# One side stage of a two-stage kernel reordered: the first chunk's inverse transform set aside in SBUF and gated later, modulation weights in other homes, two convolution inputs requested sooner, a second product group on GpSimd

## The chip, the cores and the metric

The kernel runs on one core of a Trainium2 chip (trn2). TensorE is PE in the rows, VectorE is DVE, ScalarE is ACT, GpSimd is POOL and SyncE, which issues most transfers, is SP. The metric is device time in microseconds (us), the median of several runs; lower is better. All stretches are in us from the start of the span.

## The reference

With S = 2048 tokens, D = 640 channels and F = 1728, everything in float32:

```python
mod = silu(c) @ w_mod                      # (1,640) @ (640, 3840), six rows of 640
sa, ca, ga, sb, cb, gb = mod               # shift, scale, gate, twice
h = layernorm(x) * (1 + ca) + sa           # x = A_q, (2048, 640)
ks = shift_conv4(A_k, A_shift_k)           # four taps along the tokens, per channel
kv = ks * A_v
y = long_conv(kv, A_ssm_k) + kv * A_ssm_D  # causal, 2048 taps per channel, by a transform
x = x + ga * (h * y)
h = layernorm(x) * (1 + cb) + sb
x = x + gb * (gelu(h^T @ w1 + b1) @ w2 + b2)^T
```

Layernorm is along the 640 channels, so the row statistics of `x` need all of `x`; the long convolution is per channel; the last line multiplies along the tokens.

## The kernel before

The first half, to about 280 us, computes the line `x = x + ga * (h * y)` in five chunks of 128 channels (`for c in range(NC)`). The rest is the token MLP, in three-pass float32r products; the change does not touch it.

The long convolution of a chunk is a transform written as small matmuls, in four named steps. `step1(side, t)` (L218) transforms the signal (side 0, from the tile `x`) or the filter (side 1, from `p`), in four quarters t; each fills one PSUM buffer that ACT copies into `z`. `f2(g)` (L237), g = 0 to 7, multiplies `z` by the tables `w`, ACT copies the filter's half to `kt`, DVE multiplies the two spectra into `p` (two products of 128x512), and `add` combines them into `y` (two 128x256 operations on POOL; those of the last group are on DVE for all chunks but the first). `i2(r)` (L267), r = 0 and 1, goes back the first half of the way, from `y` through PSUM into `z`; `i1(half)` (L287) the second half, from `z` into PSUM. `gate(c, ps, half)` then multiplies the result with the modulated layernorm of that chunk, the tile A1 (in `aux`, columns 2048 to 4095), and POOL adds the product to the rows of `x`, which are held in `xa` and `xb`.

A1 comes from `a1_ops(c)` (L298): 16 ACT operations (x - mean) / deviation, called `ac`, and DVE operations that scale and shift with the mod rows G1 and G0, called `po`.

The chunks overlap. While chunk c passes through f2, DVE prepares the next signals: `kv_ops(g)` (L180) makes eight operations of 128x512 for each of four groups of rows g (taps, sums, the product with v), written to `x`. A list `fill` holds them and `dv(n)` runs n of them at a place in DVE's program. For chunk 2, prepared while chunk 1 is in f2, group 1 is POOL's (`late`) and groups 0, 2 and 3 are DVE's. The loop over g keeps two halves of `p` by turns: the products of group g overwrite what the addition of group g - 2 read.

Only the first chunk carries the start of the modulation. `load_q` (L527) gathers the rows of `x` with eight indirect transfers on POOL's queue, DVE takes the statistics (`bn_stats`, L594), `rstd` (L335) makes the deviations with a square root on ACT and a correction on DVE, `mod_part(ps, kk, place)` (L350) multiplies silu(c) with one fifth of three mod rows' weights into the PSUM buffer `tap`, `mod_sum` (L357) copies the three rows to SBUF, and `mod_row(i)` (L362) broadcasts one to 128 partitions; rows 0 and 1 become G0 and G1 on ACT, and row 2, the gate, is multiplied into both on DVE. The five fifths of the weights are loaded into `homes` (L536) by SP. The later mod rows are loaded the same way while chunk 3 ends, and are used in chunk 4.

Each engine runs its own program in the order in which the Python code calls it, and the order is all written by hand. An engine that waits holds up what stands behind it, and so does SP's queue: a transfer waits there until its target is free, and until the transfer eight places ahead in SP's list has landed. `perm(c)` (L169) brings the filter from `aux` into `p`, after POOL's `perm_add(c)` has added ssm_D to it. `load_ks(c)` loads the filter into `aux` columns 0 to 2047, where k of chunk 1 has lain before.

## Time and profile before

| | us |
|---|---|
| median of 3 runs | 663.41 (660.25 to 663.55) |
| the profiled execution's own time | 661.62 |
| its span | 659.8 |
| PE busy | 615.0 (93%) |
| DVE busy | 536.9 (81%) |
| ACT busy | 328.6 (50%) |
| POOL busy | 135.1 (20%) |

Busy time by stretch, with the TensorE clock that was granted (1.00 is full speed):

| stretch, us | what runs there | PE busy | DVE busy | ACT busy | POOL busy | clock |
|---|---|---|---|---|---|---|
| 0 to 58 | inputs, chunk 0 in step1 and f2 | 43.25 | 43.71 | 24.86 | 44.01 | 1.00 |
| 58 to 82 | chunk 1 in step1, chunk 0 in i2, mod parts | 21.35 | 20.80 | 13.03 | 4.11 | 1.00 |
| 82 to 100 | mod rows, chunk 0 in i1, its gate | 13.88 | 15.78 | 13.07 | 8.13 | 1.00 |
| 100 to 124 | chunk 1 in f2 | 20.08 | 23.55 | 13.73 | 19.20 | 1.00 |
| 124 to 148 | chunk 1 in i2 and i1 | 23.27 | 19.70 | 13.18 | 4.78 | 1.00 |
| 148 to 192 | chunk 2 | 42.52 | 38.60 | 25.89 | 15.38 | 1.00 |
| 192 to 236 | chunk 3 | 42.16 | 30.96 | 24.62 | 15.28 | 0.96 |
| 236 to 280 | chunk 4 | 39.61 | 37.21 | 25.18 | 10.07 | 0.96 |
| 280 to 342 | start of the MLP | 55.28 | 55.67 | 48.36 | 0.00 | 0.97 |
| 342 to 660 | MLP | 313.60 | 250.93 | 126.68 | 14.16 | 1.00 |

A row of a timeline gives the start, the duration, engine, line, operation, the tile written and those read, the count that was merged into the row, and in brackets the idle time before it and what ended that. The same work repeats from chunk to chunk, so a stretch of one chunk can be held beside the same stretch of another.

### The profile page before, as it was taken

Reading aid. Unit: us, or ns where it says so; the run is one execution under the profiler, and the core shown is the slowest. Engines: PE = TensorE matmul, PEld = TensorE weight load, DVE = VectorE, ACT = ScalarE, POOL = GpSimd, SP = SyncE. Lnnn points to the kernel's source line nnn. Section 1 sums busy time; section 2 is a strip of 40 time slices with the busy share of each in tenths; the row PEclk is TensorE's granted clock in tenths of the full one; section 3 lists DMA queues with packets and bytes.
Section 4 is the critical chain, followed back from the end, with each engine's and each line's share of the span. In section 5 each row is a group of like instructions: output and inputs, shape, how many; then the busy total and the mean of one; then the engine's idle time right before and its main releaser. Section 6 shows DMA issues by size and latency. Waiting matters only on the chain.

```text
span 659.8 us, 20919 instructions
## 1 busy us (share of the span) xinstructions
PE 615.0 (93%) x9061; PEld 582.7 (88%) x9061; DVE 536.9 (81%) x930; ACT 328.6 (50%) x538; POOL 135.1 (20%) x151
## 2 busy tenths in 40 slices
PE   6878878999999999879999999999999999999997
PEld 2767667899998997779897999999999999999997
DVE  5879889979889369889979866575899689888895
ACT  0654575746747456377885553345443143333331
POOL 5786048325036043000000000000000520000000
PEclk9999999999999899889999999999999999999999
DMA  9999298465525046260318352245922636346601
GB/s 182 213 339 403 67 188 170 107 113 134 88 68 181 4 107 206 49 142 11 65 33 229 111 148 70 63 123 159 291 80 65 194 108 183 111 122 182 182 31 40
DMA packets 172188, 88.46 MB, mean 134 GB/s; under 512 B 92126, under 2 KB 163328, under 8 KB 172096
## 3 DMA queue, kind: packets, MB, share of 16 engines
q1 hardware_dynamic: 163628, 80.29, 46.6%
q0 software_dynamic: 1408, 5.52, 2.1%
q10 hardware_dynamic: 7060, 1.32, 1.3%
q8 instruction: 71, 1.16, 0.8%
q14 instruction: 21, 0.17, 0.1%
HBM read 73.01 MB, written 14.09 MB: 132 GB/s over the span
## 4 chain that ended last, share of the span: by engine, by line
PE 64%; DVE 17%; DMA 6%; ACT 5%; POOL 4%; issue 3%; ACTq 1%; SPq 0%; DVEq 0%; POOLq 0%
PE pst L1253 16%; PE pst L940 12%; PE pst L448 7%; PE pst L1330 7%; PE pst L226 7%; PE pst L274 5%; PE pst L245 4%; DVE p L59 3%; PE pst L294 2%; POOL t L59 2%; DVE aux L59 2%; DMA y<-in_A_ssm_k_dram 1%; ACT z L283 1%; PE pst L996 1%; DVE sm L553 1%
## 5 line engine op out<-in xcount | busy, mean ns | idle before, releaser
L245 PE MATMUL pst<-z,w 128*64 128x64 f32 x2560 | 80.4, 223 | 12.7 <-DVE p L59 6.6
L245 PEld LDWEIGHTS pst<-z,w 128*64 128x64 f32 x2560 | 77.5, 138 | 16.2 <-issue 12.3
L232 ACT ACTIVATE z<-pst 128x1024 f32<-128x1024 f32 (+2 forms) x45 | 43.4, 978 | 38.8 <-PE pst L226 38.6
L59 POOL TENSOR_TENSOR y<-p 128x256 f32<-128x256 f32 x72 | 51.0, 739 | 32.3 <-DVE p L59 32.0
L59 DVE TENSOR_TENSOR p<-pst,kt 128x512 f32<-128x512 f32 x80 | 51.1, 682 | 7.7 <-ACT kt L249 4.2
L249 ACT ACTIVATE kt<-pst 128x512 f32<-128x512 f32 x40 | 23.9, 598 | 38.2 <-PE pst L245 18.7
L226 PE MATMUL pst<-v,p 128*64 128x128 f32 x640 | 36.9, 274 | 5.3 <-ACT p L171 3.9
L1253 PE MATMUL pst<-r_z,m_w 128*128 128x320 f32 x222 | 41.6, 310 | 0.1
L274 PEld LDWEIGHTS pst<-v,y 32*128 32x128 f32 x1280 | 38.0, 187 | 3.5 <-issue 3.1
L226 PEld LDWEIGHTS pst<-v,p 128*64 128x64 f32 x640 | 34.8, 137 | 6.9 <-ACT p L171 4.9
L274 PE MATMUL pst<-v,y 32*128 32x64 f32 x1280 | 39.9, 273 | 0.6 <-issue 0.5
L59 DVE TENSOR_TENSOR s_w<-s_w,s_w 128x768 fp32r<-128x768 f32 (+1 forms) x26 | 24.6, 947 | 18.9 <-ACT s_w L924 14.2
L924 ACT ACTIVATE s_w<-s_w 128x768 fp32r<-128x768 f32 (+1 forms) x26 | 21.8, 837 | 35.7 <-PE pst L940 10.8
L1241 ACT ACTIVATE m_w<-m_v 128x896 fp32r<-128x896 f32 x24 | 22.7, 951 | 32.3 <-PE pst L1253 16.8
L59 DVE TENSOR_TENSOR tap<-tap,kt 128x512 f32<-128x512 f32 x51 | 35.5, 697 | 1.3
L226 PE MATMUL pst<-v,x 128*64 128x128 f32 x512 | 32.4, 282 | 2.9 <-issue 1.7
L1253 PEld LDWEIGHTS pst<-r_z,m_w 128*128 128x128 f32 x222 | 34.8, 188 | 0.4 <-DVE m_w L59 0.4
L448 PE MATMUL pst<-r_z,wb 128*128 128x320 f32 x180 | 29.6, 322 | 4.3 <-DVE aux L59 2.7
L448 PEld LDWEIGHTS pst<-r_z,wb 128*128 128x128 f32 x180 | 28.1, 197 | 5.6 <-DVE aux L59 2.9
L226 PEld LDWEIGHTS pst<-v,x 128*64 128x64 f32 x512 | 29.2, 142 | 4.0 <-issue 2.5
L283 ACT ACTIVATE z<-pst 128x512 f32<-128x512 f32 x38 | 20.9, 646 | 20.2 <-PE pst L274 20.2
L59 DVE TENSOR_TENSOR m_w<-m_v,m_w 128x896 fp32r<-128x896 f32 x24 | 27.9, 1167 | 3.3 <-ACT m_w L1241 2.9
(365 smaller groups left out, 1545.7 us busy)
## 6 DMA issues: line engine op xcount, KB each, us to landing
m_x<-xs SPq DMA_DIRECT2D x28, 160.0 KB
out_dram<-m_x SPq DMA_DIRECT2D x28, 160.0 KB
aux<-in_A_ssm_k_dram SPq DMA_DIRECT2D x8, 512.0 KB
m_v<-in_B_w_dram SPq DMA_DIRECT2D x9, 448.0 KB
in<-in_w_mod_dram SPq DMA_DIRECT2D x4, 960.0 KB
x<-in_B_w_dram SPq DMA_DIRECT2D x7, 448.0 KB
s_w<-in_B_w_dram SPq DMA_DIRECT2D x16, 192.0 KB
in<-in_A_v_dram SPq DMA_DIRECT2D x22, 128.0 KB
```

The lines of the kernel that those rows point to most:

```text
L59: TT = lambda eng, o, a, b, op: eng.tensor_tensor(o, a, b, op=op)
L226: pe.matmul(ps[64 * ri:64 * ri + 64, o:o + 255:2], lhs, F1[:, 128 * ri:128 * ri + 128], start=True, stop=True)
L232: act.activation(Z[:, side, t, :, k0:k1], ps.rearrange("p (a k e) -> p a k e", a=4, e=2)[:, :, k0:k1], AF.Copy)
L245: pe.matmul(ps[64 * h:64 * h + 64, o:o + 64], W2[k1 // 32][:, 2 * (k1 % 32) + ri], rhs, start=True, stop=True)
L249: act.activation(kt.rearrange("p (m i) -> p m i", i=32), pv[:, :, 1], AF.Copy)
L274: pe.matmul(pp[qd // 2][:, o:o + 64], Y[p, ri, i:i + 2].rearrange("p i k -> p (i k)"), V2[p, 64 * ri:64 * ri + 64], start=ri == 0, stop=ri ...
L283: act.activation(o, i, AF.Copy)
L448: pe.matmul(ps[0:m, h, 0:320], w_.bitcast(F32R), r_[:, 320 * h:320 * h + 320].bitcast(F32R), start=first and i == 0, stop=last and i == 2)
L940: pe.matmul(o, w_.bitcast(F32R), r_.bitcast(F32R), start=first and k == 0, stop=last and k == 2)
L1241: act.activation(W[n][0].bitcast(F32R), A[p, w_], AF.Copy)
L1253: pe.matmul(bank[n], w[:, i].bitcast(F32R), r.bitcast(F32R), start=i == 0 and k == 0, stop=i == 6 and k == 2)
L1330: pe.matmul(acc[s][:, h, 0:320], w[:, f_].bitcast(F32R), u[r + h].bitcast(F32R), start=f_ == 0 and k == 0, stop=f_ == NF - 1 and k == 2)
```

## The change

It has five parts, all in the first half.

1. POOL's queue before f2 of chunk 0: the taps of chunk 2 and the four small transfers of c, b2 and b1 go from POOL to SP, so the indirect gathers stand first on POOL. Two of five weight parts get other homes (`in` and `g` with `t`) and are requested before f2 of chunk 0; the third lies in `aux` from column 2048 on, so columns 0 to 2047 are free for the filter of chunk 1, which is requested (with k of chunk 2) right after step1 of chunk 1 begins.
2. Mod parts 0, 1 and 2 stand between the quarters of step1 on PE; the deviations are made before i2(1); a dummy Sqrt stands early on ACT.
3. The inverse of chunk 0 (`i1`) is copied by ACT into A1, in place of a DVE product from PSUM; the modulated layernorm of chunk 0 is written into the tile `x` instead (named XA). i1 and its copies stand ahead of `mod_row`; the gate is then `po`, a DVE product of two SBUF tiles, and POOL's addition.
4. Of the product groups of chunk 2, POOL takes 1 and 3, DVE 0 and 2. Seven operations of group 1 stand on POOL ahead of the gate's additions, its last behind them, then two of group 3; the other six stand in f2 of chunk 1. A one-column POOL operation ahead of group 1 reads DVE's copies of the table `v`.
5. The later mod weights are requested in nine pieces (`mod_third`) from f2 of chunk 3 on, each behind a one-column ACT write into its home, in place of three loads at the end of that chunk.

```diff
+    XA = X.rearrange("p (j d) -> p j d", j=16)
 def a1_ops(c):
+        A = A1 if c else XA
-        ac = [lambda j=j: act.activation(A1[:, j], XR(j, DC * c, DC), AF.Identity, scale=rs1[:, j:j + 1],
+        ac = [lambda j=j: act.activation(A[:, j], XR(j, DC * c, DC), AF.Identity, scale=rs1[:, j:j + 1],
...
-    homes = [T_v1[:, 2048:3968], T_in[:, 192:2112], T_aux[:, 0:1920], T_in[:, 2240:4160], P[:, 0:1920]]
+    homes = [T_in[:, 192:2112], None, T_aux[:, 2048:3968], T_in[:, 2240:4160], P[:, 0:1920]]
+    pl = [three(t) if t is not None else [G1, T_t[:, 0:640], T_t[:, 640:1280]] for t in homes]
-    load_taps(2, pool)
+    load_q((4, 5, 6, 7))
...
-        pool.dma_start(stg[o:o + t.shape[0], :], t)
+        sync.dma_start(stg[o:o + t.shape[0], :], t)
-    load_q((4, 5, 6, 7))
-    mod_load(0, 1, homes[1])
+    load_taps(2)
+    mod_load(0, 0, homes[0])
+    for j in range(3):
+        sync.dma_start(pl[1][j], dram(w_mod, 128 * 6 * D + 640 * j, [[6 * D, 128], [1, 640]]))
+    turns = {0: 6, 1: 7, 4: 8, 6: 0, 7: 1}
+    def mod_third(n):
...
+        kk, j = divmod(n, 3)
+        act.activation(pl[kk][j][:, 0:1], epsc, AF.Copy)
+        sync.dma_start(pl[kk][j], dram(w_mod, 128 * kk * 6 * D + 640 * (3 + j), [[6 * D, 128], [1, 640]]))
...
-                    mod_load(0, 0, homes[0])
-            if c == 1 and 1 < g < 6:
+            if c == 1 and g < 6:
                 late[g + 2]()
+            if cn == NC - 1 and g in turns:
+                mod_third(turns[g])
...
+            load_D(1)
             step1(0, 0)
...
+            act.activation(tm[:, 0:1], epsc, AF.Sqrt)
+            load_ks(1)
+            mod_part(tap, 0, pl[0])
+            load_halo(2)
+            load_k(2, 0, n=2)
             step1(0, 1)
+            mod_part(tap, 1, pl[1])
             i2(0)
             step1(0, 2)
+            mod_part(tap, 2, pl[2])
+            rstd(rs1, nm1, 0, 16)
...
+            pool.tensor_scalar(tm[64:128, 0:1], T_v1[64:128, 0:1], 1.0, None, op0=ALU.mult)
+            late = kv_ops(1, pool)
+            run(late[:7])
             i2(1)
-            k0 = step1(0, 3, True)
-            for kk in range(4):
+            step1(0, 3)
+            for kk in (3, 4):
                 mod_part(tap, kk, pl[kk])
...
+            run(ac[0:4])
             mod_sum(tap, T_kt[:, 0:640])
+            taps()
+            perm(1)
+            fill.extend(kv(3, ((0, 0), (2, 1, 2))))
+            dv(7)
+            for half in range(2):
+                act.activation(A1[:, 8 * half:8 * half + 8].rearrange("p j (y e c) -> p e (j y) c", e=2, c=2),
+                               i1(half).rearrange("p (e y c) -> p e y c", e=2, c=2), AF.Copy)
             for i in range(3):
                 mod_row(i, T_kt[:, 0:640])
             run(ac[4:16])
-            taps()
-            run(po[0:2])
-            perm(1)
-            fill.extend(kv(3, ((0, 0), (2,), (3, 1, 2, 3))))
+            for half in range(2):
+                y, x = A1[:, 8 * half:8 * half + 8], XH[half][:, :, 0:DC]
+                run(po[2 * half:2 * half + 2])
+                TT(dve, y, y, XA[:, 8 * half:8 * half + 8], ALU.mult)
+                TT(pool, x, x, y, ALU.add)
+            late[7]()
+            late = kv_ops(3, pool)
+            run(late[:2])
```

How this stands on the engines, at three places. First PE behind f2 of chunk 0: `pst<-v,x` is a quarter of step1 of chunk 1, `pst<-v,g` the transpose that carries c, `pst<-v,y` i2(0), and `tap<-` a mod part. Before:

```order
L226 MATMUL pst_740<-v,x 64x128 x16
L605 MATMUL pst_758<-v,g 128x36
L226 MATMUL pst_762<-v,x 64x128 x16
L274 MATMUL pst_780<-v,y 128x64 x2
L274 MATMUL pst_781<-v,y 128x64 x2
```

The same place on PE in the changed kernel:

```order
L227 MATMUL pst_744<-v,x 64x128 x16
L623 MATMUL pst_762<-v,g 128x36
L356 MATMUL tap<-in,sm 32x320 x6
L227 MATMUL pst_779<-v,x 64x128 x16
L356 MATMUL tap<-g,sm 32x320
L356 MATMUL tap<-t,sm 32x320 x2
```

Mod part 0, which reads silu(c), now stands ahead of the second quarter, and mod part 1 ahead of i2(0).

Second ACT, from the copies of i2(1) (`z<-pst`, 128x512) to the first copy of step1 of the next filter (`z<-pst`, 128x4x128x2, the last row of each): `sm<-sm 128x16` is the square root, `x<-xa` or `aux<-xa` is `ac`, `kt<-tap` is mod_sum, `tap<-rows` the taps, `p<-aux` perm(1), `g<-pst` the mod rows. Before:

```order
L283 ACTIVATE z<-pst_869 128x512 x2
L338 ACT_TABLE_LOAD
L338 ACTIVATE sm<-sm 128x16
L301 ACTIVATE aux<-xa,sm 128x128 x4
L358 ACTIVATE kt<-tap 96x640
L232 ACTIVATE z<-pst_938 128x4x128x2
L372 ACTIVATE g<-pst_1018 128x640
L374 ACTIVATE g<-pst_1022 128x640
L301 ACTIVATE aux<-xa,sm 128x128 x4
L301 ACTIVATE aux<-xb,sm 128x128 x8
L177 ACTIVATE tap<-rows 128x256
L171 ACTIVATE p<-aux 128x16x2x32 x2
```

In the changed kernel, where `aux<-pst` are the two new copies of i1:

```order
L284 ACTIVATE z<-pst_919 128x512 x2
L233 ACTIVATE z<-pst_988 128x4x128x2
L303 ACTIVATE x<-xa,sm 128x128 x4
L360 ACTIVATE kt<-tap 96x640
L178 ACTIVATE tap<-rows 128x256
L172 ACTIVATE p<-aux 128x16x2x32 x2
L662 ACTIVATE aux<-pst_1045 128x2x256x2
L662 ACTIVATE aux<-pst_1111 128x2x256x2
L374 ACTIVATE g<-pst_1177 128x640
L376 ACTIVATE g<-pst_1181 128x640
L303 ACTIVATE x<-xa,sm 128x128 x4
L303 ACTIVATE x<-xb,sm 128x128 x8
```

The taps, perm(1) and the two new copies stand ahead of the mod rows now; the square root is further up.

Third POOL, from the end of chunk 0's f2 into chunk 1's: `t<-in,t`, `t<-t` and `x<-t,in` are kv operations, `xa<-xa,aux` and `xb<-xb,aux` the gate's additions, `y<-p` the additions of f2. Before:

```order
L59 TENSOR_TENSOR aux<-aux,rows 1x64 x2
L59 TENSOR_TENSOR xa<-xa,aux 128x8x128
L59 TENSOR_TENSOR xb<-xb,aux 128x8x128
L59 TENSOR_TENSOR t<-in,t 128x512 x2
L59 TENSOR_TENSOR t<-t 128x512
L59 TENSOR_TENSOR t<-in,t 128x512
L59 TENSOR_TENSOR y<-p 128x8x32 x2
```

In the changed kernel, from the end of the seven operations of group 1 on:

```order
L59 TENSOR_TENSOR t<-t 128x512
L59 TENSOR_TENSOR xa<-xa,aux 128x8x128
L59 TENSOR_TENSOR xb<-xb,aux 128x8x128
L59 TENSOR_TENSOR x<-t,in 128x8x32x2
L59 TENSOR_TENSOR t<-in,t 128x512 x2
L59 TENSOR_TENSOR t<-t 128x512
L59 TENSOR_TENSOR t<-in,t 128x512
L59 TENSOR_TENSOR y<-p 128x8x32 x2
```

Between the gate's additions and the first addition of f2 stand five kv operations, where four stood; behind that the two lists agree to the end of chunk 1's f2.

More of the change, by code (lines that the diff above doesn't have):

```diff
@@ L586, in mixer_kernel @@
                 perm_add(cn)
+            if cn == NC - 1 and g in turns:
+                mod_third(turns[g])
+            if c == 1 and g == 5:
+                kv_loads(3, 3)
         pend_m()
@@ L664, in mixer_kernel @@
             dv(7 if cn is not None else 8)
+            if cn == NC - 1:
+                mod_third(2)
             i2(0)
@@ L682, in mixer_kernel @@
         if cn == NC - 1:
[L683 to L689 removed]
+            mod_third(5)
+        for half in range(2 if c else 0):
             ps = i1(half)
[L691 removed]
+            if half:
                 dv(3)
[L693 removed]
+            else:
                 k0 = step1(1, 0, True)
[L695 to L696 removed]
             gate(c, ps, half)
[L698 to L700 removed]
         spill(c)
```

54 lines of the change are left out of this document (18 added, 36 removed).

## The prediction

> **What bounds the kernel now.** I read the page first, for the span and the chain of waits.
>
> ```profile
> span 659.8 us, 20919 instructions
> PE 64%; DVE 17%; DMA 6%; ACT 5%; POOL 4%; issue 3%; ACTq 1%; SPq 0%; DVEq 0%; POOLq 0%
> ```
>
> PE carries the chain, but 17% of it is DVE, with POOL and ACT behind. The change touches the stretch from 36 to 124 us and chunk 3, so I took PE's timeline there next.
>
> ```profile
> 58.49 1.97 PE L226 MATMUL pst<-v,x 128*64 128x128 f32 x32 [0.83 <-DVE x L59]
> 68.29 1.91 PE L226 MATMUL pst<-v,x 128*64 128x128 f32 x30 [1.66 <-issue]
> 75.92 1.28 PE L354 MATMUL tap<-v,sm 128*32 128x320 f32 x12
> 80.25 1.25 PE L354 MATMUL tap<-p,sm 128*32 128x320 f32 x12
> 100.53 10.20 PE L245 MATMUL pst<-z,w 128*64 128x64 f32 x320 [0.49 <-ACT z L232]
> 120.20 3.71 PE L226 MATMUL pst<-v,x 128*64 128x128 f32 x64 [0.44 <-DVE p L59]
> 123.85 3.80 PE L274 MATMUL pst<-v,y 32*128 32x64 f32 x128
> 147.89 5.82 PE L245 MATMUL pst<-z,w 128*64 128x64 f32 x192 [0.49 <-ACT z L232]
> 163.95 3.69 PE L226 MATMUL pst<-v,x 128*64 128x128 f32 x64
> ```
>
> Three landmarks: chunk 1's step1 begins at 58.49, its f2 at 100.53 and its i2(0) at 123.85. What follows 123.85 the change leaves alone until chunk 3, so the gain is what i2(0) of chunk 1 moves, plus chunk 3. f2 took 19.67 us (100.53 to 120.20), and in chunk 2 16.06 (147.89 to 163.95), so other engines hold PE in chunk 1.
>
> **POOL's queue before f2 of chunk 0.** The waits of 34 to 60 us, then POOL's timeline:
>
> ```profile
> DVE p L59 <- POOL y L59: 3.4, 4, 1.7
> 35.95 1.09 POOL L152 DMA_DIRECT2D rows<-in_A_shift_k_dram  x2
> 39.42 1.03 POOL L531 DMA_INDIRECT xb<-in_A_q_dram,rows_of  x1 [0.30 <-issue]
> 42.66 0.94 POOL L531 DMA_INDIRECT xb<-in_A_q_dram,rows_of  x1 [0.94 <-DMA rows<-in_A_shift_k_dram]
> ```
>
> DVE's products wait for POOL's additions, which stand behind the gathers, and those behind six small transfers. Without these the first gather moves from 39.42 to 36.3 (0.30 of issue after 35.95), and the wait of 0.94 for the taps goes too. Then DVE sets the pace. Of its 3.4 us of waiting behind POOL nearly all goes, as 3.1 of transfers and 0.94 of wait leave POOL's queue ahead of it: I take 3.0 us, so step1 begins at 55.5. Ends: 0, if the gathers still hold the additions (everything below is then 3.0 later), and 3.4, the whole wait. SP takes the small transfers, which are read only when step1 begins.
>
> **PE and ACT up to the mod rows.** ACT's timeline:
>
> ```profile
> 62.95 0.21 ACT L607 ACTIVATE sm<-sm 128x5 f32<-128x5 f32 x1
> 74.11 2.21 ACT L283 ACTIVATE z<-pst 128x512 f32<-128x512 f32 x4 [2.82 <-PE pst L274]
> 79.53 1.65 ACT L301 ACTIVATE aux<-xa,sm 128x128 f32<-128x128 f32 x4 [1.59 <-DVE sm L343]
> 81.56 0.70 ACT L358 ACTIVATE kt<-tap 96x640 f32<-96x640 f32 x1 [0.38 <-PE tap L354]
> 84.29 0.70 ACT L374 ACTIVATE g<-pst 128x640 f32<-128x640 f32 x1
> 89.50 0.63 ACT L177 ACTIVATE tap<-rows 128x256 f32<-128x256 f32 x1
> 90.06 2.19 ACT L171 ACTIVATE p<-aux 128x1024 f32<-128x1024 f32 x2
> 93.27 1.09 ACT L232 ACTIVATE z<-pst 128x1024 f32<-128x1024 f32 x1 [1.02 <-PE pst L226]
> ```
>
> Mod part 0 needs silu(c), which ended at 63.16, 4.67 after step1 began. PE is done with the first quarter and the transpose after 2.1 and so waits about 2.65 that it did not wait before. Three mod parts now stand ahead of i2(1): 1.1 each (five in the 5.58 from 75.92 to 81.50), 3.3. The stall of 1.66 plus 0.25 in front of the third quarter has no releaser; I leave it out, and keep it for the upper end. i2(1) ended 15.6 after step1 began, where ACT's row at 74.11 was released; now 15.6 - 1.9 + 2.65 + 3.3 = 19.65, so at 75.15. Behind PE's new wait for silu(c) stand the other quarters and i2, and for those waits ACT.
>
> From there ACT is the chain, because the mod rows now stand behind everything: i2(1) 2.2, the last quarter 1.1, `ac` 1.65, mod_sum 0.7, taps 0.65, perm(1) 2.2, two copies of i1, mod rows 1.4. The copies are not in the trace: they move 128x1024 from PSUM like `z<-pst`, 1.09 each (nearest row; ends 1.09 and 1.23, the price of DVE's product below), so 2.2. Sum 12.1: G1 is there at 87.2, against 84.99. The dummy Sqrt takes a table load out of this chain and lies under PE's matmuls. Four more `ac` (1.64) put the first half of A at 88.8. The filter of chunk 1, which perm reads, is requested before step1's second quarter now, and has some 20 us to land.
>
> **The gate.** DVE's and POOL's timeline:
>
> ```profile
> 75.48 0.21 DVE L595 BATCH_NORM_AGGREGATE sm<-sm 128x2 f32<-128x12 f32 x1
> 79.53 2.46 DVE L622 TENSOR_SCALAR v<-v 64x2048 f32<-64x2048 f32 x2
> 86.55 2.52 DVE L59 TENSOR_TENSOR aux<-aux,g 128x1024 f32<-128x1024 f32 x2 [0.29 <-ACT aux L301]
> 89.17 1.23 DVE L59 TENSOR_TENSOR aux<-pst,aux 128x1024 f32<-128x1024 f32 x1
> 90.31 4.54 DVE L59 TENSOR_TENSOR aux<-aux,g 128x1024 f32<-128x1024 f32 x2
> 90.57 3.21 POOL L59 TENSOR_TENSOR xa<-xa,aux 128x1024 f32<-128x1024 f32 x1 [2.58 <-DVE aux L59]
> 96.33 2.37 POOL L59 TENSOR_TENSOR xb<-xb,aux 128x1024 f32<-128x1024 f32 x1 [2.55 <-DVE aux L59]
> ```
>
> Two DVE operations that took 2.52 took 4.54 while POOL's addition ran, and that addition 3.21 instead of 2.37: one engine stood while the other worked. The Trainium skill, "SBUF — State Buffer", section "SBUF: two separate sides", has a rule for it: a DVE operation with two SBUF inputs and a GpSimd operation that reads SBUF exclude each other for whole instructions. The trace agrees by the two rows above. By that rule the new product, from two SBUF tiles in place of PSUM and SBUF, joins the operations that exclude, and the sum is the next one only if POOL is idle when DVE's pair starts, and each POOL operation still running then adds its length.
>
> POOL's group 1 waits for DVE's copies of `v`, and the gate's additions stand behind it. The statistics end 3.0 earlier, at 72.7; the square root (0.3, its table loaded before) and DVE's correction (1.6, to 79.53 in the trace) follow, and the copies (2.46 and 1.23) end at 78.3. One table copy (1.1) and seven operations of 1.3 (98.66 below) end at 88.7, just as DVE's pair begins at 88.8. So 2.52 + 1.23 after 88.8 puts the first gate product at 92.5, against 90.40. From there the order of operations is as before, and from 90.40 to the end of POOL's second addition (98.70) it took 8.3. So POOL is through at 100.8, 2.1 later than before. f2 of chunk 1 itself can begin sooner: step1 of the filter needs perm and free PSUM, and ACT copies its quarters behind the twelve `ac` from about 92, so f2 begins near 95.5 instead of 100.53.
>
> **f2 of chunk 1.** From the groups of 100 to 124 us, and POOL's timeline:
>
> ```profile
> L59 POOL TENSOR_TENSOR y<-p 128x256 f32<-128x256 f32 x14 | 10.0, 743 | 2.9 <-DVE p L59 2.8
> L59 DVE TENSOR_TENSOR p<-pst,kt 128x512 f32<-128x512 f32 x16 | 10.1, 681 | 0.0
> 98.66 2.51 POOL L59 TENSOR_TENSOR t<-in,t 128x512 f32<-128x512 f32 x2
> 119.54 2.81 POOL L59 TENSOR_TENSOR y<-p 128x256 f32<-128x256 f32 x4 [1.01 <-DVE p L59]
> ```
>
> DVE never waited in this f2: it was the bound, with 16 kv operations among its products, and the change takes 8 away (0.7 each, 5.6) and does 7 more ahead of it. But POOL gets them. From 98.70 to 122.35 POOL took 23.65, 2.8 of it waiting for DVE. It now has one kv operation more (1.3; nine instead of eight) and no waits: 23.65 - 2.8 + 1.3 = 22.15, after 100.8, so 122.95. Every product of group g waits for the addition of group g - 2, and four kv operations of group 3 stand ahead of the first addition. So PE, five us early, is held by POOL through this f2. The last product and DVE's last addition follow, and i2(0) begins at about 123.5 instead of 123.85: gain 0.3. Ends: -1.6 with the stall of issue back, +2.5 (90.40 to 98.70 in 6.1 instead of 8.3) if POOL and DVE do not exclude each other once.
>
> **Chunk 3.**
>
> ```profile
> 203.14 3.99 SPq L347 DMA_DIRECT2D in<-in_w_mod_dram x2
> 211.98 1.32 PE L274 MATMUL pst<-v,y 32*128 32x64 f32 x34
> 213.83 3.22 PE L274 MATMUL pst<-v,y 32*128 32x64 f32 x94 [0.52 <-issue]
> 216.98 3.26 PE L226 MATMUL pst<-v,x 128*64 128x128 f32 x32
> 216.00:218.00 2.00, 2.00 (x35) 1.88 (x33) 1.99 (x4) 1.14 (x3) 0.00 (x0) 0.57 0.00 0
> ```
>
> Here the weights arrive in one burst; right behind it PE stalls 0.52 in i2(0), and the granted clock is 0.57 (the last number but two) in the two us shown. i2(0) took 5.07 (211.98 to 217.05) against 3.80 in chunk 1, and the quarter behind it 3.26 against 1.97: 2.55 together. Requested in pieces from 193 on, the burst is gone. The gain lies between 0 and 2.55; the stall of 0.52 I expect gone, of the slow clock I count half, as two later stretches (0.96 and 0.97 in the table above) have slow spells without such loads: 1.3. The Trainium skill, "TensorE: Matmul & The Clock Gate", section "What's actually happening", says that the clock is halved by a free-running activity window. The trace agrees in size (0.57); by that alone the loads would not matter and this term would be 0.5. The nine ACT writes (0.2 each by the 128x5 one above) fall where ACT waits for PE, and SP's queue behind them holds only chunk 3's writes to DRAM: nothing.
>
> **The sum.** 0.3 + 1.3 = 1.6 less: 660.0 against the profiled execution's 661.62. The median of three stands 1.8 above that one, and all four average 662.2. From this I take 661.0. A measurement can tell about 0.5% of this kernel, 3.3 us, from no change.
>
> **The rivals.** First, faster: POOL does not hold f2. If POOL's additions come in time, f2 runs at chunk 2's 16.06 from 95.5, and i2(0) starts at 95.5 + 16.06 + 3.7 = 115.3, 8.5 earlier; with chunk 3 some 652. For it speaks that PE is ready 5 us early and DVE relieved; against it, that POOL's 23.65 holds only 2.8 of waiting. In part it may come true, if POOL's chain begins before 98. Chance 0.2.
>
> Second, slower: the gathers of x come late. From the windows:
>
> ```profile
> 50.00:55.00 5.00, 3.98 (x118) 3.62 (x114) 3.84 (x7) 2.44 (x4) 4.67 (x7) 1.00 1.02 412
> ```
>
> The transfers run at their limit (share 1.02, 412 GB/s) while the gathers are under way, and a weight part (128 rows of 3x640, 0.98 MB, 2.4 us at that rate) is now requested ahead of most gathers. If bn_stats waits so much and the 3.0 of the first term is lost, it ends 5.4 later than I count, at 78.1. Then the square root on ACT holds the copies of i2(1), DVE's copies of `v` end at 83.7 instead of 78.3, and i1 and the mod rows move by 3.4. POOL's group 1, which reads those copies first, ends at 94.0 instead of 88.7, beside DVE's pair of SBUF inputs: 1.3 more of exclusion. i2(0) begins at 123.5 + 4.7 = 128.2, and the time is 664.7, or 666 without the gain in chunk 3. It decides from bn_stats ending after 75, where POOL's group 1 begins to reach into `po`. For it: the full share. Against: the gathers were never waited for by bn_stats before. Chance 0.2.
>
> Third, the change doesn't do what it says: the weights' pieces and the first term move nothing that PE waits for, and the other edits trade places: 661.6 to 663. Chance 0.1. The forecast has 0.5; its own range is 657.5 to 664.5.
>
> **The numbers.** Range 654 to 667: from the middle of the first rival to beyond the second. Faster by over 0.5%: the first rival and a fifth of the forecast, 0.31. Slower by over 0.5%: most of the second rival, 0.17. The rest, 0.52, within.
>
> **What would show it.** Right: step1 of chunk 1 begins at 55 to 56; PE waits 2 to 3 us for ACT ahead of mod part 0; POOL's second gate addition ends at 100 to 102, later than before; f2 of chunk 1 begins at 95 to 96 with PE waiting for DVE in it and DVE's products for POOL; i2(0) at 123 to 125. Wrong: f2 of chunk 1 in under 18 us would mean that POOL does not hold it; DVE idle in bn_stats for a transfer would mean the second rival; a clock of 1.00 in chunk 3 makes that term 2.5.

## The result, and the profile after

The changed kernel took 668.2 us (median of 20 runs, 663.0 to 676.8); the kernel before took 662.8 (20 runs). The ratio is 1.0065, 95% interval 1.0037 to 1.0094: slower by 0.65%, where 661.0 was forecast and 667 was the upper end of the range. Here and below medians are of all runs, ratios of the undisturbed ones. The profiled execution of the changed kernel took 671.65, with a span of 669.9 and a mean granted clock of 0.966; that of the kernel before had 659.8 and 0.992, and in it PE had no slow spell from 34 to 145 us, which none of the other 19 profiles of this study repeats.

The page's head and the shares of the chain in the changed kernel:

```profile
span 669.9 us, 20943 instructions
PE 65%; DVE 16%; ACT 6%; issue 4%; POOL 3%; DMA 3%; SPq 1%; ACTq 0%; POOLq 0%; DVEq 0%
```

The shares say little: the same engines as before. The places do. PE's timeline of the changed kernel at the landmarks of the prediction (start, busy, and in brackets the wait ahead of the row and what ended it):

```profile
36.74 5.82 PE L246 MATMUL pst<-z,w 128*64 128x64 f32 x192 [0.49 <-ACT z L233]
50.66 5.50 PE L246 MATMUL pst<-z,w 128*64 128x64 f32 x127 [2.54 <-issue]
58.76 1.97 PE L227 MATMUL pst<-v,x 128*64 128x128 f32 x32
63.47 1.46 PE L356 MATMUL tap<-in,sm 128*32 128x320 f32 x12 [2.56 <-ACT sm L625]
64.85 3.48 PE L227 MATMUL pst<-v,x 128*64 128x128 f32 x32
76.30 3.80 PE L275 MATMUL pst<-v,y 32*128 32x64 f32 x128
101.23 5.82 PE L246 MATMUL pst<-z,w 128*64 128x64 f32 x192 [0.49 <-ACT z L233]
115.00 5.50 PE L246 MATMUL pst<-z,w 128*64 128x64 f32 x128 [3.18 <-DVE p L59]
128.80 4.02 PE L275 MATMUL pst<-v,y 32*128 32x64 f32 x128 [0.51 <-DVE y L59]
```

step1 of chunk 1 begins at 58.76 (forecast 55.5; 58.49 before), f2 at 101.23 (95.5; 100.53 before) and i2(0) at 128.80 (123.5; 123.85 before). Three waits stand out: 2.54 without a releaser ("<-issue") in f2 of chunk 0, where the longest of the kernel before was 1.78, the forecast one for silu(c), 2.56, and 3.18 for DVE's products in chunk 1's f2. Behind each of the three, rows that should be short are long: step1's second quarter took 3.48 where the first took 1.97.

The windows of the changed kernel at those places (the last three columns are the granted clock, the transfers' share and their GB/s):

```profile
52.00:54.00 2.00, 2.00 (x44) 2.00 (x42) 0.00 (x0) 0.18 (x1) 1.01 (x2) 0.50 1.01 403
62.00:64.00 2.00, 0.53 (x6) 0.42 (x9) 1.93 (x8) 1.97 (x3) 0.00 (x0) 1.00 1.03 391
66.00:68.00 2.00, 2.00 (x22) 2.00 (x20) 1.93 (x7) 0.00 (x0) 0.00 (x0) 0.50 1.04 397
116.00:118.00 2.00, 2.00 (x43) 2.00 (x42) 1.92 (x3) 0.33 (x1) 2.00 (x4) 0.50 0.41 93
```

Each of the three waits is followed by a spell at half clock. The waits of 34 to 60 us in the changed kernel (engine, what it did, whom it waited for: us in total, times, longest):

```profile
ACT kt L250 <- issue: 4.2, 1, 4.2
PE pst L246 <- issue: 4.0, 3, 2.5
DVE p L59 <- POOL y L59: 0.3, 1, 0.3
```

DVE's wait for POOL, 3.4 before, is gone as forecast. But PE and ACT now stand longer without a releaser (PE 4.0 against 3.2), and step1 begins no sooner. In part that is this execution's later start: f2 of chunk 0 began at 36.74 instead of 34.90, so step1 stands 22.02 behind it instead of 23.59; but the second profile of the kernel before, below, has 21.75. The rest of the chain in the changed kernel's timeline, on ACT, DVE and POOL:

```profile
91.97 0.70 ACT L376 ACTIVATE g<-pst 128x640 f32<-128x640 f32 x1 [1.11 <-PE pst L367]
94.25 2.48 DVE L59 TENSOR_TENSOR x<-x,g 128x1024 f32<-128x1024 f32 x2 [0.60 <-ACT x L303]
96.76 1.23 DVE L59 TENSOR_TENSOR aux<-aux,x 128x1024 f32<-128x1024 f32 x1
97.91 4.52 DVE L59 TENSOR_TENSOR x<-x,g 128x1024 f32<-128x1024 f32 x2
98.12 3.22 POOL L59 TENSOR_TENSOR xa<-xa,aux 128x1024 f32<-128x1024 f32 x1 [4.85 <-ACT x L303]
103.83 2.39 POOL L59 TENSOR_TENSOR xb<-xb,aux 128x1024 f32<-128x1024 f32 x1 [2.49 <-DVE aux L59]
124.01 4.20 POOL L59 TENSOR_TENSOR y<-p 128x256 f32<-128x256 f32 x6
```

From the first gate product's end (97.99) to the end of POOL's second gate addition (106.22) it took 8.23, forecast 8.3; from there to the end of POOL's list (128.21) 22.0, forecast 22.15. Every step stands in its forecast order and length; the whole chain stands 5.4 too late.

### The profile page after: what moved, and what is told of

The parts are those of the page before. It is cut to its first block, busy times and chain, and to the rows that moved or that the text cites. A ratio compares the mean times of both kernels' runs of the same rounds, so it can differ in the third digit from the quotient of the medians.

```text
span 669.9 us, 20943 instructions
## 1 busy us (share of the span) xinstructions
PE 627.6 (94%) x9061; PEld 593.5 (89%) x9061; DVE 532.2 (79%) x922; ACT 330.8 (49%) x550; POOL 142.9 (21%) x154
## 3 DMA queue, kind: packets, MB, share of 16 engines
q8 instruction: 71, 1.16, 0.7%
## 4 chain that ended last, share of the span: by engine, by line
PE 65%; DVE 16%; ACT 6%; issue 4%; POOL 3%; DMA 3%; SPq 1%; ACTq 0%; POOLq 0%; DVEq 0%
PE pst L1281 16%; PE pst L968 11%; PE pst L450 7%; PE pst L1358 7%; PE pst L227 6%; PE pst L275 6%; PE pst L246 6%; PE pst L295 2%; DVE p L59 2%; POOL t L59 2%; ACT z L284 2%; PE pst L1024 1%; POOL y L59 1%; DVE x L59 1%; PE tap L356 1%
## 5 line engine op out<-in xcount | busy, mean ns | idle before, releaser
L246 PE MATMUL pst<-z,w 128*64 128x64 f32 x2560 | 81.9, 227 | 13.3 <-DVE p L59 6.9
L246 PEld LDWEIGHTS pst<-z,w 128*64 128x64 f32 x2560 | 79.7, 142 | 16.1 <-issue 11.7
L275 PEld LDWEIGHTS pst<-v,y 32*128 32x128 f32 x1280 | 41.0, 201 | 4.8 <-issue 3.4
L227 PE MATMUL pst<-v,p 128*64 128x128 f32 x640 | 39.8, 287 | 4.0 <-ACT p L172 4.0
L275 PE MATMUL pst<-v,y 32*128 32x64 f32 x1280 | 42.9, 287 | 0.6 <-DVE y L59 0.5
L227 PEld LDWEIGHTS pst<-v,p 128*64 128x64 f32 x640 | 37.9, 146 | 5.6 <-ACT p L172 4.8
L59 DVE TENSOR_TENSOR tap<-tap,kt 128x512 f32<-128x512 f32 x48 | 33.4, 696 | 1.2
L59 DVE TENSOR_TENSOR m_w<-m_v,m_w 128x896 fp32r<-128x896 f32 x24 | 27.9, 1167 | 3.3 <-ACT m_w L1269 2.9
```

What stands on the lines that cost most here:

```text
L59: TT = lambda eng, o, a, b, op: eng.tensor_tensor(o, a, b, op=op)
L227: pe.matmul(ps[64 * ri:64 * ri + 64, o:o + 255:2], lhs, F1[:, 128 * ri:128 * ri + 128], start=True, stop=True)
L246: pe.matmul(ps[64 * h:64 * h + 64, o:o + 64], W2[k1 // 32][:, 2 * (k1 % 32) + ri], rhs, start=True, stop=True)
L275: pe.matmul(pp[qd // 2][:, o:o + 64], Y[p, ri, i:i + 2].rearrange("p i k -> p (i k)"), V2[p, 64 * ri:64 * ri + 64], start=ri == 0, stop=ri ...
```

## The experiments

Four theories. **CHAIN**: the gate ends later and POOL's longer list holds chunk 1's f2. **CLOCK**: PE's new waits of 2.5 to 3.2 us bring half-clock spells. **FETCH**: the waits without a releaser, while the transfers are full, hold f2 of chunk 0, whatever POOL's queue holds. **PIECES**: the weights' pieces in chunk 3 cost time.

**The same again, and the pieces.** These runs are the changed kernel again, the same without the pieces, the kernel before with the pieces alone, and the kernel before again. The edit for the second, and its opposite for the third (in part):

```diff
-            if cn == NC - 1 and g in turns:
-                mod_third(turns[g])
...
-            mod_third(5)
+            for kk in range(2):
+                mod_load(3, kk, (T_in[:, 0:1920], T_in[:, 1920:3840])[kk])
+            for j in range(3):
+                sync.dma_start(pl[2][j], dram(w_mod, 256 * 6 * D + 640 * (3 + j), [[6 * D, 128], [1, 640]]))
```

> The changed kernel once more, for a second profile. Theory CHAIN (the gate of chunk 0 and POOL's list hold chunk 1): i2(0) of chunk 1 begins 4 to 5 us later than in the kernel before (123.85), at 127 to 129, and POOL's products' wait on it is there again. Theory CLOCK (PE's new waits make the granted clock drop): the same waits of 2.5 to 3.2 us on PE (for silu(c) near 61, for DVE's products near 112) are each followed by some 3.4 us at about 0.5, and the whole is 0.4 to 0.9% slower. If the slow spells lie elsewhere or are missing while the time is the same, CLOCK falls.

> The changed kernel with part 5 undone (the later mod weights in three loads at the end of chunk 3, as before). CHAIN: part 5 was worth 1.3 us at most 2.5, so this is 0 to 2.5 us slower than the changed kernel, some 0.8 to 1.0% slower than before. A third theory, PIECES (the nine pieces and ACT's one-column writes cost time in chunks 3 and 4): this is faster than the changed kernel by 2 us or more.

> The kernel before with part 5 alone (the later mod weights in nine pieces). CHAIN and the prediction: 0.5 to 2.5 us faster than before, i2(0) of chunk 3 without the stall. PIECES: slower than before by 2 us or more, with the slow clock in chunk 4. CLOCK: within 1 us of before, as no wait on PE is changed.

> The kernel before once more, for a second profile. CLOCK: no waits of over 2 us on PE between 36 and 124 us and a clock of 1.00 there; slow spells only from chunk 3 to the start of the MLP, at other places than in the first profile. CHAIN: i2(0) of chunk 1 within 1.5 us of 123.85, f2 of chunk 0 and step1 as in the first profile.

Measured: the changed kernel 668.64, ratio 1.0108 [1.0064, 1.0152]; without the pieces 669.05, 1.0112 [1.0066, 1.0157]; the pieces alone 662.74, 1.0020 [0.9985, 1.0054]; the kernel before 665.51 in one run. The pieces are worth nothing in time, so PIECES falls, and so does the prediction's 1.3. They do remove the stall in i2(0) of chunk 3: over all 20 profiles it is there in four of the seven without the pieces, as in the second one of the kernel before, and in none of the 13 with them, where i2(0) took 3.80.

```profile
218.23 2.90 PE L274 MATMUL pst<-v,y 32*128 32x64 f32 x94 [0.52 <-issue]
```

The slow clock behind it was the first execution's own: the quarter behind i2(0) took 3.26 there and 1.97 in the other 19. The second profile of the kernel before misses what was expected of it: three waits of 2.1 to 2.3 without a releaser, spells at half clock from 71 and 88 us, and i2(0) of chunk 1 at 128.94, as late as in the changed kernel. So one pair of profiles doesn't give the loss. Counted from the start of f2 of chunk 0, i2(0) of chunk 1 begins 89.0 and 90.1 later in the two profiles of the kernel before, 92.1 and 93.2 in the two of the changed one.

**CLOCK, twice, and CHAIN.** Two ways to end PE's wait for silu(c): mod part 0 behind the second quarter, or five useless matmuls in the wait; and group 3's kv operations given back to DVE (each in part):

```diff
# after_swap
+            step1(0, 1)
             mod_part(tap, 0, pl[0])
             load_halo(2)
             load_k(2, 0, n=2)
-            step1(0, 1)
# after_dummy
+            for _ in range(5):
+                pe.matmul(tap[:, 0:512], T_w2[0][:, 0:128], T_w2[0][:, 0:512], start=True, stop=True)
             mod_part(tap, 0, pl[0])
# after_dve3
-            if c == 1 and g < 6:
-                late[g + 2]()
...
-            fill.extend(kv(3, ((0, 0), (2, 1, 2))))
+            fill.extend(kv(3, ((0, 0), (2,), (3, 1, 2, 3))))
...
-            late = kv_ops(3, pool)
-            run(late[:2])
```

> The changed kernel with one edit: mod part 0 behind step1's second quarter, so that PE works while ACT makes silu(c). CHAIN: PE's wait there shrinks from 2.56 to about 0.6, and everything behind it on PE and ACT moves up by 1.9; i2(0) of chunk 1 begins 1.9 earlier than in the changed kernel (129.5 on the mean of three profiles), 0.3% faster. CLOCK: the slow spell that began near 64 goes too, 1.5 more: 3 to 4 us in all, 0.5%.

> The changed kernel with five useless 128x512 matmuls on PE in its wait for silu(c), into PSUM that is overwritten next; they leave the wait as long as it was. CLOCK: no slow spell behind it (1.00 from 62 to 70), the second quarter of step1 in 1.97 instead of 3.5, i2(0) of chunk 1 some 1.5 earlier. CHAIN: no change of time, as no operation waits less; if the slow spell is there in spite of a busy PE, CLOCK falls.

> The changed kernel with product group 3 of chunk 2 on DVE again, so POOL has one group. CHAIN: POOL's list behind the gate's additions loses eight operations (10.4 us), DVE's products no longer wait for POOL (0 instead of 7 us), but DVE takes the eight (5.7 us) and becomes the bound: from the gate's last product on DVE (103.7) 17 kv operations of 0.72, 16 products of 0.64 and the last addition, 24 us, put i2(0) of chunk 1 at about 127.5 to 128.5, 1 us earlier at best. If the time stays, the second group on POOL bought nothing and cost nothing.

After the swap, 665.60, ratio 1.0045 [1.0011, 1.0079]. PE's row ahead of mod part 0 in its timeline, and the window behind it:

```profile
63.14 1.35 PE L356 MATMUL tap<-in,sm 128*32 128x320 f32 x12 [0.33 <-ACT sm L625]
```

```profile
64.00:68.00 4.00, 4.00 (x107) 3.25 (x104) 3.86 (x14) 1.55 (x3) 0.00 (x0) 1.00 1.03 395
```

The wait is 0.33 instead of 2.56 and the clock 1.00 where it was 0.50; i2(0) of chunk 1 begins at 128.33, 1.2 earlier than the mean of three that the expectation names, not 1.9. With the useless matmuls, 667.98, ratio 1.0057 [1.0021, 1.0094], the timeline shows:

```profile
62.61 4.56 PE L629 MATMUL tap<-w 128*128 128x512 f32 x10
68.30 1.97 PE L227 MATMUL pst<-v,x 128*64 128x128 f32 x32
```

The second quarter took 1.97 again, at the same place in the order: what slowed it was that PE had stood idle. One profile could be chance, but over the seven profiles with the wait five have a spell right behind it, over the six in which PE works there none. The matmuls took 2 us more than the wait, and so gave the gain away. With group 3 on DVE, 664.66, ratio 1.0022 [0.9992, 1.0052], PE's timeline and a window where the changed kernel's 3.18 and its spell were:

```profile
112.35 2.08 PE L246 MATMUL pst<-z,w 128*64 128x64 f32 x64 [1.16 <-DVE p L59]
115.60 2.09 PE L246 MATMUL pst<-z,w 128*64 128x64 f32 x64 [1.17 <-DVE p L59]
127.55 3.80 PE L275 MATMUL pst<-v,y 32*128 32x64 f32 x128
```

```profile
116.00:120.00 4.00, 2.84 (x97) 2.73 (x94) 3.90 (x8) 2.11 (x6) 1.86 (x3) 1.00 0.80 178
```

DVE sets an even pace, no wait is longer than 1.2, no spell follows, and 3.5 us of the median are back: the second group on POOL is the costliest of the parts that were tried alone.

**Both at once, and the rows ahead.** The swap with group 3 on DVE; and, on top, the mod rows and the last twelve `ac` ahead of the taps (in part; the same lines further down go):

```diff
             mod_sum(tap, T_kt[:, 0:640])
+            for i in range(3):
+                mod_row(i, T_kt[:, 0:640])
+            run(ac[4:16])
             taps()
```

> The changed kernel with mod part 0 behind step1's second quarter and group 3 given back to DVE, both at once. CHAIN and CLOCK together: each alone gave back about 3 and 4 us (665.6 and 664.7), at different places (the silu wait of 2.6 and its spell at 64-68; the wait of 3.0 for DVE and its spell at 114-120). If they add, 661 to 662, ratio 0.997 to 1.000, with PE's longest wait for an engine between 58 and 130 under 2 us and i2(0) of chunk 1 at 90 or less behind the start of f2 of chunk 0. If the gate's chain alone holds i2(0), the two overlap and the time is 664 to 665, like the better one of them.

> The same, and the mod rows and the last twelve normalizations ahead of taps, perm and the two copies of i1 on ACT, so that G1 is there some 5 us sooner (ACT's 0.65 + 2.2 + 2.2). CHAIN, if the gate's end is what holds chunk 1's f2: POOL's second gate addition ends at 101 instead of 105 to 107, and the time falls by 2 to 4 against the kernel with both edits, to 658 to 660. If perm, which is 3 us later, holds f2 of chunk 1 in its place: f2 begins at 98 instead of 95 and the time doesn't move, or rises by 1.

Measured: 663.75, ratio 1.0025 [0.9987, 1.0063], and 665.17, 1.0053 [1.0018, 1.0088]. The two edits overlap: both together are hardly better than group 3 alone, and level with the kernel before. The rows ahead helped nothing, through the edit's own order: G1's product on DVE began at 87.58, 4.5 sooner than in the changed kernel, but the seven kv operations that stand ahead of `po` on DVE read the taps and now waited 4.17 for them, so that POOL's first gate addition began at 102.16 instead of 98.21 without this edit. What an earlier gate is worth was not measured.

**What is chain and what is clock.** Each run lists its span and mean granted clock. One line through the runs of all 18 kernels that the ratios use, with a level for each kernel and a common slope, has 3.55 us for 0.01 of clock (residual 1.6 us), and splits each loss into a part at equal clock and a part by the clock (± is a 95% interval):

| kernel | runs | at equal clock, against before | by the clock |
|---|---|---|---|
| changed (both series) | 23 | +3.4 ± 0.7 | +1.3 ± 0.9 |
| mod part 0 behind the second quarter | 12 | +3.0 ± 1.0 | +0.3 ± 1.2 |
| group 3 on DVE | 12 | +1.1 ± 1.0 | +0.5 ± 0.7 |
| both | 12 | +0.7 ± 1.0 | +0.5 ± 1.1 |
| useless matmuls in the wait | 11 | +4.1 ± 1.0 | +0.5 ± 1.2 |

Group 3 on DVE takes 2.3 (± 1.1) of the 3.4 at equal clock: that is POOL's second group. The swap leaves the part at equal clock as it was. Somewhat over a quarter of the loss goes by the clock in this fit, but the swap's 0.3 is not clear of the 1.3 by these intervals, and the pieces alone have +1.4 too. A loss by the clock is shown in the rows behind the wait and not in the whole time.

A length that hardly varies says the same of the chain. From the first matmul of chunk 1's f2 to i2(0) it took 23.2 to 23.3 in all seven profiles of the kernel before and its edits, 26.4 to 27.9 in all eight of the changed kernel and its edits with both groups on POOL, with a slow spell in it or without, and 24.2 to 24.7 with group 3 on DVE, but for two profiles with further edits (28.2 with the rows ahead, 26.3 with the hold below).

**FETCH.** First POOL's queue alone: the kernel before with the gathers first on POOL and the small transfers on SP (in part).

```diff
-    load_taps(2, pool)
+    load_q((4, 5, 6, 7))
...
-        pool.dma_start(stg[o:o + t.shape[0], :], t)
+        sync.dma_start(stg[o:o + t.shape[0], :], t)
...
-    load_q((4, 5, 6, 7))
+    load_taps(2)
```

> The kernel before with part 1's edit of POOL's queue alone: the gathers first on POOL, the small transfers on SP. The prediction's first term: DVE waits for POOL in f2 of chunk 0 0.4 us or less instead of 3.4, step1 of chunk 1 begins up to 3.0 earlier, and the time is 2 to 3 us lower. A rival, FETCH (PE's stalls without a releaser, some 2 us each in this f2, hold it whatever POOL does): the waits go and step1 begins within 1 us of before.

Measured: 662.91, ratio 0.9997 [0.9965, 1.0030]. Its waits of 34 to 60 us, and step1 in its timeline:

```profile
PE pst L245 <- issue: 5.5, 3, 2.5
DVE p L59 <- POOL y L59: 2.6, 1, 2.6
```

```profile
58.62 1.97 PE L226 MATMUL pst<-v,x 128*64 128x128 f32 x32
```

Of DVE's waiting for POOL one wait of 2.6 stayed, where 0.4 was expected, and step1 begins 21.72 behind the start of f2 of chunk 0 (23.59 and 21.75 in the two profiles of the kernel before). The queue's order is worth nothing by itself. Then fewer bytes: a third of each mod weight part, used three times, which leaves two thirds of those weights out of the sum (edit: width 640 for 1920, and one place for three).

> The kernel before with a third of each mod weight part loaded and used three times (the mod values are then other ones): 3.3 MB fewer of the 14.4 MB that move between 30 and 85 us, 1.3 MB of it while f2 of chunk 0 runs. FETCH, if PE's and ACT's stalls without a releaser are instruction fetches behind a full DMA: they shrink from 5.5 to 7 us to under 4, and step1 of chunk 1 begins at 20 or less behind the start of f2 of chunk 0, instead of 21.7 to 23.6; time 660 to 661. If the stalls have nothing to do with the transfers: 5.5 to 7 us as before, step1 at 21.7 or later, time 662 to 663.

> The changed kernel with the same third of each mod weight part. FETCH: DVE's wait for POOL is gone already, so with the stalls shrunk too, step1 of chunk 1 begins at 19 to 20 behind the start of f2 of chunk 0 (22.0 in the changed kernel), which is the first term of the prediction come back; but PE still waits 2.6 for silu(c), POOL's list still holds chunk 1, and the time falls by 2 at most, to 666 to 667. If the stalls have nothing to do with the transfers: 22.0 and 668 to 669.

Measured: 658.90, ratio 0.9952 [0.9925, 0.9978], and 666.76, 1.0074 [1.0035, 1.0113]. The kernel before gains 3.9, but not in f2: PE's stalls there are 3.5 (3.2 and 6.0 in its two profiles), step1 still begins at 58.49, and what goes are the stalls behind it (i2(1) ends 13.8 after step1's start instead of 15.6 in its first profile). In the changed kernel step1 stays at 58.69. So the transfers were taken out of f2 itself: the first two weight parts and c_v1 requested behind it (in part; the request of the other part, ahead of f2, goes too).

```diff
-                if g == 4:
-                    sync.dma_start(T_v1[:, 0:2048], c_v1, max_dma_last_dim=2048)
-                    mod_load(0, 0, homes[0])
...
-            for kk in range(2, 5):
+            for kk in range(5):
                 mod_load(0, kk, homes[kk])
+            sync.dma_start(T_v1[:, 0:2048], c_v1, max_dma_last_dim=2048)
```

> The kernel before with the first two mod weight parts and c_v1 (2.96 MB) requested behind f2 of chunk 0 instead of in it. FETCH, full transfers hold PE's and ACT's instructions: the gathers' 5.2 MB are done some 5 to 7 us sooner, the stalls in f2 fall from 5.5 to under 3, and step1 of chunk 1 begins at 56 to 57 (58.5 to 60.6 before); behind it the 5.9 MB of weights keep the transfers full until 72, with stalls of 1 to 3 there, so the time is 660 to 663. If f2's own work or the gathers pin step1: 58.5 to 59 again, time 662 to 664.

> The same in the changed kernel. FETCH: DVE's wait for POOL is gone here, so step1 begins at 55 to 56.5 (58.8), which is the prediction's first term; PE's wait for silu(c) stays, as mod part 0 needs silu(c) later than its weights; from 668 to 665 to 667. If the gathers pin step1: 58.5 to 59 and 668 to 669.

> The changed kernel with part 0 behind the second quarter, group 3 on DVE, and these late loads. FETCH: 2 to 3 less than the 663.75 without the late loads, 661 to 662, ratio 0.995 to 1.000, step1 at 55 to 56.5. If the gathers pin step1: 663 to 664.

Measured: 661.63, ratio 0.9990 [0.9955, 1.0026]; 673.30, 1.0134 [1.0073, 1.0195]; 665.47, 1.0034 [0.9999, 1.0068]. In the changed kernel the edit missed: SP asked for the parts at 38.5 and 40.6 (39.8 and 41.1 without it), as nothing holds its queue there, and only c_v1 moved. By the fit above its runs lie 3.1 (± 1.6) over the kernel before at equal clock, as the changed kernel does; the rest of the 673.30 is clock. In the kernel before it took hold. Its windows, its waits of 34 to 62 us and step1 in its timeline:

```profile
42.00:46.00 4.00, 2.51 (x83) 2.54 (x85) 3.75 (x7) 3.01 (x4) 1.78 (x2) 1.00 0.87 303
46.00:50.00 4.00, 1.87 (x64) 1.76 (x60) 1.85 (x3) 1.76 (x3) 3.51 (x6) 1.00 0.84 286
```

```profile
PE pst L245 <- DVE p L59: 5.9, 4, 2.8
DVE p L59 <- POOL y L59: 4.2, 4, 2.4
```

```profile
59.75 3.52 PE L226 MATMUL pst<-v,x 128*64 128x128 f32 x32 [2.58 <-DVE x L59]
```

PE has no wait without a releaser left in f2 that is worth a row; the waits for POOL are there in their place. Whether that is the transfers' doing is not separated here: their share is lower at 40 to 50 us, but 0.8 to 1.2 again from there on, and PE, which waits 5.9 for DVE, is slower. The last runs take both away: in the kernel before, POOL's queue as in the change together with the late loads; in the changed kernel, the late loads behind one ACT write that holds SP, whose first lines are:

```diff
+            act.activation(pl[0][0][:, 0:1], epsc, AF.Copy)
             mod_load(0, 0, homes[0])
```

> The kernel before with both: gathers first on POOL's queue and the small transfers on SP, and the first two weight parts and c_v1 behind f2 of chunk 0. FETCH: with POOL's waits (3.4 to 4.3) and the stalls without a releaser (5.5) both gone, f2 of chunk 0 runs at DVE's pace and step1 of chunk 1 begins 20 or less behind the start of f2 (21.7 with POOL's queue alone, 24.9 with the late loads alone); the time is 659 to 661, ratio 0.994 to 0.999. If something else pins step1: 21.7 or more again, 662 to 663.

> The changed kernel with one ACT write of a column into the first weight part's place, behind f2's last copy, so that SP asks for all five parts and c_v1 only then. FETCH: step1 begins 20 or less behind the start of f2 (22 in the changed kernel), the prediction's first term of 3 us come back; behind it the weights arrive 2.4 apart from 59 on, so mod part 0 waits for its weights as long as for silu(c), and stalls of 1 to 3 lie in i2; time 664 to 667. If the full transfers don't pin step1: 21.5 to 22, 667 to 669.

> The same hold, with part 0 behind the second quarter and group 3 on DVE. FETCH: step1 20 or less behind the start of f2, and 1 to 3 less than 663.75 (both edits without the hold): 661 to 663. If not: 663 to 666.

Measured: 666.55, ratio 1.0046 [1.0006, 1.0085]; 673.25, 1.0190 [1.0139, 1.0241]; 668.56, 1.0120 [1.0063, 1.0176]. All three miss. PE's timeline of the first, and its windows:

```profile
40.76 0.34 PE L245 MATMUL pst<-z,w 128*64 128x64 f32 x4 [0.41 <-issue]
42.20 0.33 PE L245 MATMUL pst<-z,w 128*64 128x64 f32 x4 [1.10 <-issue]
43.66 9.50 PE L245 MATMUL pst<-z,w 128*64 128x64 f32 x253 [0.50 <-issue]
60.72 1.97 PE L226 MATMUL pst<-v,x 128*64 128x128 f32 x32
```

```profile
38.00:42.00 4.00, 1.48 (x21) 1.03 (x18) 3.09 (x5) 0.94 (x1) 3.08 (x4) 1.00 1.03 372
50.00:54.00 4.00, 3.47 (x110) 3.34 (x107) 3.45 (x6) 2.39 (x4) 3.82 (x5) 1.00 0.81 257
```

The stalls moved to the front of f2: from 38 to 44, while the gathers alone fill the transfers, PE got four or five matmuls at a time with 0.4 to 1.1 between them, then ran 9.5 us without a break, at a share of 0.94 to 1.03 until 49 us and 0.58 to 0.86 behind that. Their sum stayed: 5.3, as 5.5 with POOL's queue alone. The held kernels lost time on top, as mod part 0 waited 3.95 (after_held_loads) for its weights.

What is shown: of 63 such waits of 0.4 us or more on PE in f2 of chunk 0, over all 20 profiles, 61 lie where the transfers' share is 0.9 or more; two, of 1.1 at 59 us in the last runs, lie where it is 0.78 and 0. This count says little, as the share is 0.9 or more in 390 of the 433 whole microseconds of this f2. The places say more: 46 of the 63 stand right behind matmul 200, 327 or 454 of f2's 512. In the changed kernel's timeline these are the row below, the one at 50.66 above and one at 56.99; the row below has the 127 matmuls between two of them.

```profile
44.23 3.89 PE L246 MATMUL pst<-z,w 128*64 128x64 f32 x127 [0.61 <-issue]
```

The page of the changed kernel counts the packets of two instruction queues apart, 71 and 21 of them, the larger one with 1.16 MB:

```profile
q8 instruction: 71, 1.16, 0.7%
```

If these 71 are PE's, there is one for 255 of its 9061 matmuls and as many weight loads; 127 matmuls with their loads are 254. PE would then stand once for each packet's worth of its program, which speaks for waits for instructions. That is still argued: the last packet of this queue ahead of each of the changed kernel's three stalls had landed 3.6 to 4.5 us before the stall's end, the short stalls at the front of f2 lie at other places, and what ends any of them is not recorded.

Where the stalls went (late loads in the kernel before), POOL's additions held step1; where the waiting for POOL went (the changed kernel), the stalls did. Why the stalls' sum is 3.4 to 5.4 in each of the 14 profiles with at most 0.3 of waiting for POOL, wherever the transfers were put, and what would have to go for step1 to begin at 55.5, stays open.

## Why the prediction was wrong

**POOL's queue (first term, −3.0): failed.** "Of its 3.4 us of waiting behind POOL nearly all goes" held (0.3 left), but the step from there to "step1 begins at 55.5" did not. "Then DVE sets the pace" took DVE for the only bound of f2, while the same view of the waits of 34 to 60 us of the kernel before has PE's stalls beside DVE's wait:

```profile
PE pst L245 <- issue: 3.2, 3, 1.8
```

I left this row out; the stall of 1.66 that I did name stands behind step1. Measured 58.76 in the profile, and the part alone moved the kernel before by −0.03% [−0.35, +0.30], with 2.6 of the waiting left there. I had named the end: 0, "everything below is then 3.0 later". That end was the case.

**PE's wait for silu(c): right in size, short in price.** 2.65 forecast, 2.56 measured. What I left out is the half-clock spell behind it, 1.5 on the second quarter (3.48 against 1.97), shown by two edits that end the wait; such a spell came in five of seven profiles, so it is a chance and no fixed price. i2(1) so ended at 80.10 instead of 75.15: 3.3 by the first term, 1.5 by the clock.

**ACT's chain to the mod rows: right.** 12.1 forecast from i2(1)'s end, 12.6 measured (80.10 to 92.67). Of this 1.11 is a wait for PE's matmuls of the mod rows, which the sum didn't have; shorter steps took back 0.6.

**The gate: right.** The first half of A at 94.25 instead of 88.8, with the delay it was handed; from the gate product on, 8.23 against 8.3. One engine stood while the other worked, as forecast: DVE's pair took 4.52 beside POOL's 3.22.

**POOL's list: right in length, wrong as a trade.** 22.0 against 22.15. "POOL gets them" was the right reading, and the first rival (POOL does not hold f2) fell: PE waited 3.18 for DVE, DVE up to 3.3 for POOL. What failed is its price: I took this as a trade that evens out, gain 0.3, as the gate's delay was to be 2.1. With the gate 5.4 later than that, the longer list had no slack (this reason is argued, as an earlier gate was not measured), and group 3 on DVE was the cheaper place, by 3.5 us in time and 2.3 at equal clock.

**Chunk 3 (−1.3): failed.** Worth 0 (1.0020 [0.9985, 1.0054] alone). The stall of 0.52 that "I expect gone" went, and the time did not fall by it. The rest was a slow spell of one execution that I read as the work of the loads behind it. (By its words the term would be 0.52 and half of the other 2.03, 1.5; 1.3 is half of 2.55.) The sentence beside that term that the Trainium skill, "TensorE: Matmul & The Clock Gate", section "What's actually happening", tells of a free-running window, by which the loads would not matter, gave 0.5 and was nearer.

**The sum.** 5.3 at i2(0) of chunk 1 (3.3 + 1.5 + 0.5 in ACT's chain) and 1.3 for chunk 3 are 6.6 of the 7.2 between forecast and median. This is the split of one profile, whose execution took 3.5 more than the median, so that it comes so near is in part luck. The place and the time of the second rival came true (128.2 and 664.7 to 666, measured 128.80 and 668.2), its mechanism did not: bn_stats never waited for a gather; it ended at 76.92, past that rival's mark of 75, because step1 itself was late. The third rival's premise came true, as the pieces and the first term moved nothing, but the other edits cost more than they gave.

## What to carry to other kernels

A wait that is removed pays only if nothing else stands behind it: where the trace shows stalls without a releaser beside full transfers, count the gain as zero until a run with that edit alone shows it. Price a new wait of 2 us or more on PE as the wait plus, in somewhat over half of the cases here, some 1.5 us of half clock behind it, and look first for an independent piece of work to put in it (here one quarter of step1 exchanged with a mod part). Before you give work to the engine that ends a chain, even when it is idle on average (21% busy here), ask how late its last part can begin: a delay ahead of it (5.4 us here) moves the whole list.

## What the runs showed of the hardware

Over all 20 profiles, between 34 and 136 us, PE's waits of 2.0 us or more that began at full clock were followed by a granted clock under 0.75 within 4 us in 29 cases of 50 (11 of 21 at 2.0 to 2.5, 11 of 19 at 2.5 to 2.9, 7 of 10 from 2.9 on). There were 50 spells in all; 35 lasted 3.3 to 3.4 us, 14 lasted 6.8 and one 13.6, that is one, two or four times the same length. No length of the wait decides alone: a wait of 2.78 and one of 3.92 had no spell behind them, and 21 of the 50 spells had only shorter waits (0.4 to 1.8) in the 4.5 us ahead, 15 of them at 81 to 98 us, in kernels of both kinds. The Trainium skill, "TensorE: Matmul & The Clock Gate", section "What's actually happening", has the clock halved after at least one idle window of about 3.4 us, free-running; the length of the spells agrees, but most of the waits that were followed by one, 2.0 to 2.9, are shorter than that.
